# Sliding-window attention with a gated feed-forward layer: one third of the gate layer of five more token groups by seven half-size products

## The chip, the cores and the metric

The kernel runs on one core of a Trainium2 chip. The metric is the device time of one execution, in microseconds (us); smaller is better. The engines that matter: TensorE (PE in the profile, PEld its weight loads), VectorE (DVE), ScalarE (ACT), GpSimd (POOL, called Pool here) and SyncE (SP), which only issues transfers. The letter q behind an engine's name stands for its instruction queue.

## The reference, cut to what matters

```python
# B, H, S, D = 8, 8, 576, 64; window 128; float32 inputs
scores = (q @ k^T) / 8 + slope_h * -|i - j|,  only for 0 <= i - j < 128
attn   = softmax(scores)
x      = (attn @ v), heads side by side       # 4608 tokens x 512
gelu   = 0.5 * g * (1 + erf(g / sqrt 2)),  g = x @ w_gate     # 512 x 1536
out    = (gelu * (x @ w_val)) @ w_out         # 1536 x 512, float32
```

## The kernel before

The 4608 tokens form nine groups g = 0 to 8 of 512 tokens. For each group the *gates* compute the hidden layer in twelve blocks f = 0 to 11 of 128 columns (`gate_val`): four matmuls of 512 columns with `wg`, four with `wv`, a Gelu by ScalarE, and a multiply by VectorE that writes block f of `hT`. Below, "hT3" is that multiply of block 3. Then `out_products` (groups 2 and up) multiplies the hidden layer by `w_out`, by Strassen's scheme in Winograd's form: seven products of half size in each direction in place of eight, P(n, a) for token quarter a. They need sums of quarters of `hT`, which `combine_left` makes in the tile `left`: four steps, s1, s2, s4 and one in place (a21). P(1,0) and P(2,0) come first and read the quarters of `hT` for the first half of the tokens, P(1,0) the even blocks and P(2,0) the odd ones, so that the last matmul of P(2,0) needs hT11.

Between these products stands the attention of batch b = g + 2 (`scores2`, exponentials by ScalarE, masks by VectorE) and the weighting of V for batch g + 1. `add` then adds the masked probabilities into `T`, from which `sums4` makes the row sums early in the next group's gates; VectorE inverts them (`RECIPROCAL r<-ps`), `gather` writes them to DRAM and `spread_dma` reads them back to all partitions. Both of these transfers are issued from ScalarE's queue, ahead of whatever ScalarE does next.

The gates of some blocks use the same scheme of seven: `gate_quad(g, f0)` makes blocks f0 to f0 + 3 of both `wg` and `wv` by 56 matmuls of 256 columns. It needs sums of weight quarters (`combine_weights`), sums of token quarters (`combine_x`, four steps t1 to t4), six copies or adds from PSUM into a float32 staging place, and four Gelus. Its last multiplies are VectorE's for the first half of the tokens and Pool's for the second (`hidden(u, 1)`). In the kernel before it serves blocks 6 to 9 of group 1, and blocks 0 to 3 and 6 to 9 of groups 7 and 8. Its seven products come in the order 1, 2, 6, 5, 7, 3, 4; 6 accumulates onto 1 after ScalarE has copied 1 out, 4 onto 7 after VectorE has read that.

Every engine's instructions run in the order of the code (`manual_schedule`); nothing is reordered by a planner. A list `put_off` holds work that is emitted inside the next group's gates. Pool issues all loads of q, k and v (`load_qk`, `load_v`, 15 transfers for each batch, line 117), SyncE the transposes of q and k and the stores. Writes of a `mark` make Pool wait until something has happened before it goes on.

Of the kernel before, what the change touches and what calls it, by code (L numbers as in the profile page):

```python
# [7 lines left out]
FP32 = mybir.dt.float32  # L8
# [15 lines left out]
RING = 2048  # L24

QUADS = {0: 0, 6: 512}
# [10 lines left out]
def kernel(  # L37
# [60 lines left out]
    emask = consts.tile([128, H, 576], BF16, name="emask")  # L98
# [131 lines left out]
    def decay(s, c):  # L230
        return emask[:, 2 * c:2 * c + 2, 192 * s:192 * s + 384]
# [4 lines left out]
    def mask(dst, m):  # L236
        nc.vector.tensor_tensor(out=dst, in0=dst, in1=m, op=ALU.mult)  # L237
# [277 lines left out]
    def values_and_sums(b, s, later=None):  # L515
# [21 lines left out]
        def scale():  # L537
            for c, a, e, _, prods in two:
                at = b * S + a
                nc.vector.tensor_tensor(  # L540
                    out=xT[:, c, at:at + e - a], in0=prods, in1=recip[b][:, c, a:e], op=ALU.mult)
# [214 lines left out]
    def flat_of(t):  # L756
        return t.rearrange("p a x -> p (a x)")

    sums_w = [flat_of(t)[:, lo:lo + 2048].rearrange("p (c f) -> p c f", c=2)
              for t, lo in ((Ps[0], 0), (Ps[0], 2048), (Ps[0], 4096), (emask, 0))]  # L760

    def combine_weights(f0, to=None, engine=nc.gpsimd):
        todo = []
        if to is None:
            to = [t[:, :, QUADS[f0]:QUADS[f0] + 512] for t in sums_w]
# [9 lines left out]
    def sums_x(g):  # L775
        t, lo = (flat_of(left[:, :, :, :].rearrange("p n i x -> p (n i) x")), 2048) if g == 1 else (
            flat_of(T), 2048 * (g % 2))
        return [t[:, lo + 512 * n:lo + 512 * n + 512].rearrange("p (c x) -> p c x", c=2) for n in range(4)]
# [5 lines left out]
    def combine_x(g, lo=0, hi=256, which=range(4)):  # L784
# [3 lines left out]
        for n in which:  # L788
            to, a, b, op = steps[n]
            nc.vector.tensor_tensor(out=to, in0=a, in1=b, op=op)  # L790

    wide = [flat_of(t)[:, 1024 * i:1024 * i + 1024].bitcast(FP32)
            for t in (qT[0], kT[0], qT[1]) for i in (0, 1)]
    gelus = [flat_of(qs[0])[:, 512 * i:512 * i + 512] for i in range(4)]

    def early_space():
        slots = [Ps[0][:, 2 * n:2 * n + 2, 64:576] for n in range(4)]
        spare = r_pool.tile([128, 4, S], FP32, name="rb")
        staging = [spare[:, n, 0:512] for n in range(4)] + [
            flat_of(vb[1])[:, 1024 * i:1024 * i + 1024].bitcast(FP32) for i in (0, 1)]  # L800
        flat = flat_of(left[:, :, :, :].rearrange("p n i x -> p (n i) x"))
        return slots, staging, [flat[:, 512 * i:512 * i + 512] for i in range(4)]

    def gate_quad(g, f0, space=None):
        if g not in hid:
# [3 lines left out]
        slots, staging, gelu_tiles = space or (  # L809
            [t[:, :, QUADS[f0]:QUADS[f0] + 512] for t in sums_w], wide, gelus)  # L810
        s1, s2, s3, s4 = slots
# [20 lines left out]
        def add_to(n, to, u):  # L832
            nc.vector.tensor_tensor(out=to[u], in0=banks[n, u], in1=to[u], op=ALU.add)  # L833

        def gelu(what, frm, u):
            nc.scalar.activation(out=gelu_tiles[2 * what + u], in_=frm[u], func=AF.Gelu)  # L836

        def both(x):
            return x.rearrange("p (e x) -> p e x", e=2)
# [5 lines left out]
        for u in (0, 1):  # L845
            copy(out=P1[u], in_=banks["x", u])
# [4 lines left out]
        for u in (0, 1):  # L851
            copy(out=U[u], in_=banks["x", u])
        P(5)
        for u in (0, 1):
            copy(out=P5[u], in_=banks["y", u])
# [10 lines left out]
        for u in (0, 1):  # L866
            nc.vector.tensor_tensor(out=hidden(u, 0), in0=both(banks["x", u]), in1=both(gelu_tiles[u]), op=ALU.mult)
            nc.gpsimd.tensor_tensor(out=hidden(u, 1), in0=both(P5[u]), in1=both(gelu_tiles[2 + u]), op=ALU.mult)  # L868
# [107 lines left out]
    def masks_of_last_blocks(lo, hi):  # L976
        nc.vector.tensor_copy(out=emask[:, lo:hi, 192:384], in_=emask[:, lo:hi, 0:192])
        nc.vector.tensor_copy(out=emask[:, lo:hi, 384:512], in_=emask[:, lo:hi, 0:128])
        for x, at in ((0, 128), (1, 0)):
            half = slice(64 * x, 64 * x + 64)  # L980
            nc.vector.tensor_copy(out=emask[half, lo:hi, 512:576], in_=emask[half, lo:hi, at:at + 64])
# [156 lines left out]
    def out_products(g):  # L1138
# [106 lines left out]
        add(b, 0, None, (2, 1))  # L1245
        put_off.append(lambda: add(b, 2))

    put_off = []

    for g in range(NG):  # L1250
        if 1 <= g < B - 2:
            transposes_dma(3 if g == 1 else g + 2)
        if g >= B - 1:
            for f in range(NF):
                if f in QUADS:
                    if g == B - 1 and f == 0:
                        sums = combine_weights(6)
                        nc.gpsimd.tensor_copy(out=mark, in_=sums_x(g)[3][0:1, 1, 254:256])
                        for do in sums[:4]:
                            do()  # L1260
                    gate_quad(g, f)
                    if g == B - 1 and f == 0:
                        for do in sums[4:]:
                            do()
# [14 lines left out]
        if g == 1:  # L1279
            space = early_space()  # L1280
            sums = combine_weights(6, space[0], nc.vector)
            for do in sums[:5]:
                do()
        for f in range(9 if g == 0 else 0, NF):
            if g == 1 and 6 <= f < 10:
                if f == 6:
                    gate_quad(1, 6, space)
                continue
            gate_val(g, f)
# [5 lines left out]
            if g == B - 2 and f == 6:  # L1295
                combine_x(g + 1, 0, 192)
            if g == B - 2 and f in (2, NF - 1):
# [88 lines left out]
```

## Time and profile before

| | |
|---|---|
| median of 3 runs | 331.38 us (330.38 to 331.44) |
| the profiled execution | 331.55 us, its span 329.7 us |
| PE, DVE, ACT, POOL busy | 321.1, 261.4, 189.2, 148.0 us |
| granted TensorE clock | 1.0 throughout |
| chain that ended last | PE 93% |

All times of single instructions are microseconds from the start of the span of the profiled execution. Groups 3, 4 and 5 are alike: their gates begin at 133.29, 167.89 and 202.44 us.

### The profile page before, as it was taken

How to read it: one execution, taken by the hardware profiler on the slowest of the kernel's cores; microseconds unless marked ns; L12 is line 12 of the kernel's file. 1: busy time of each engine (PE TensorE's matmuls, PEld its weight loads, DVE VectorE, ACT ScalarE, POOL GpSimd, SP SyncE). 2: the span in 40 equal slices, each digit the busy share in tenths (PEclk: the TensorE clock that was granted, in tenths of full speed). 3: DMA queues.
4: the chain of work that ended last, by engine and by line, in shares of the span. 5: the costliest groups of instructions: out<-in, count | busy, mean ns of one | idle time of the engine just before them, and what ended most of it. 6: DMA issues, size and time to landing. Idle time of an engine off the chain costs nothing.

```text
span 329.7 us, 9178 instructions
## 1 busy us (share of the span) xinstructions
PE 321.1 (97%) x3664; PEld 204.4 (62%) x3664; DVE 261.4 (79%) x545; ACT 189.2 (57%) x371; POOL 148.0 (45%) x181
## 2 busy tenths in 40 slices
PE   8999999999999998999999999999999999999996
PEld 6566646574654466545854486447744787788764
DVE  7788686878779975989699769986899776886692
ACT  7974688567798365424842385237623247636641
POOL 5965589293095085105900392014014448910550
PEclk9999999999999999999999999999999999999999
DMA  8999999999999979969994599649201430003003
GB/s 214 168 195 191 202 170 168 145 190 154 135 179 154 165 139 196 167 151 166 173 184 128 138 155 156 153 139 133 99 33 45 104 130 2 0 2 128 2 0 127
DMA packets 149918, 43.54 MB, mean 132 GB/s; under 512 B 133588, under 2 KB 142964, under 8 KB 149876
## 3 DMA queue, kind: packets, MB, share of 16 engines
q0 software_dynamic: 107456, 18.10, 72.4%
q1 hardware_dynamic: 39104, 18.55, 26.7%
q10 hardware_dynamic: 3316, 6.32, 8.2%
q8 instruction: 28, 0.46, 0.5%
q14 instruction: 14, 0.11, 0.1%
HBM read 43.65 MB, written 9.53 MB: 161 GB/s over the span
## 4 chain that ended last, share of the span: by engine, by line
PE 93%; ACT 3%; DMA 1%; issue 1%; DVE 1%; ACTq 0%; DVEq 0%
PE ps L650 44%; PE ps L753 19%; PE ps L825 9%; PE ps L504 5%; PE ps L687 5%; PE ps L303 2%; PE ps L221 2%; PE ps L707 2%; ACT P L234 2%; DMA rd<-r 1%; PE ps L78 1%; PE ps L440 1%; PE ps L159 1%; PE ps L989 1%; PE ps L341 1%
## 5 line engine op out<-in xcount | busy, mean ns | idle before, releaser
L657 ACT ACTIVATE gelu<-ps 128x512 bf16<-128x512 f32 (+3 forms) x97 | 53.5, 557 | 80.1 <-PE ps L650 68.8
L650 PE MATMUL ps<-xT,wg 128*128 128x512 bf16 (+4 forms) x392 | 92.3, 357 | 0.0
L650 PE MATMUL ps<-xT,wv 128*128 128x512 bf16 (+4 forms) x392 | 92.2, 357 | 0.0
L658 DVE TENSOR_TENSOR hT<-ps,gelu 128x512 bf16<-128x512 f32 (+3 forms) x97 | 59.2, 633 | 17.6 <-PE ps L650 13.0
L650 PEld LDWEIGHTS <-wv 128*128 128x128 bf16 x392 | 37.2, 98 | 39.3 <-DVE xT L558 0.5
L650 PEld LDWEIGHTS <-wg 128*128 128x128 bf16 x392 | 36.5, 98 | 36.4
L234 ACT ACTIVATE P<-ps 128x512 bf16<-128x512 f32 (+1 forms) x108 | 52.3, 576 | 4.2 <-PE ps L221 2.1
L237 DVE TENSOR_TENSOR P<-P,emask 128x768 bf16<-128x768 bf16 x60 | 31.9, 553 | 7.2 <-ACT P L234 5.4
L753 PEld LDWEIGHTS <-hT 128*128 128x128 bf16 x336 | 31.9, 97 | 7.4 <-DVE hT L658 0.7
L117 POOL DMA_DIRECT2D vb<-in_v_dram x40 | 33.9, 888 | 3.6 <-DMA wo<-in_moe_w_out_dram 1.0
L1331 POOL COPY mark<-hT 1x2 bf16<-1x2 bf16 x4 | 1.5, 366 | 73.1 <-DVE hT L658 73.1
L117 POOL DMA_DIRECT2D ks<-in_k_dram x30 | 25.4, 889 | 4.4 <-DMA qs<-in_q_dram 4.2
L753 PEld LDWEIGHTS <-left 128*128 128x128 bf16 x252 | 24.2, 98 | 4.9 <-issue 1.6
L117 POOL DMA_DIRECT2D qs<-in_q_dram x30 | 25.2, 856 | 1.8 <-issue 1.2
L753 PE MATMUL ps<-right,hT 128*128 128x256 bf16 x168 | 22.2, 272 | 0.2 <-DVE osb L895 0.2
L753 PE MATMUL ps<-right,left 128*128 128x256 bf16 x168 | 20.6, 273 | 1.5 <-issue 1.5
L753 PE MATMUL ps<-wo,hT 128*128 128x256 bf16 x168 | 21.2, 273 | 0.4 <-DVE hT L658 0.4
L504 PE MATMUL ps<-P,vb 64*64 64x192 bf16 (+2 forms) x752 | 18.2, 221 | 1.6 <-issue 0.8
L868 POOL TENSOR_TENSOR hT<-qT,qs 128x512 bf16<-128x512 f32 x8 | 9.2, 1169 | 21.4 <-ACT qs L836 21.4
L504 PEld LDWEIGHTS <-vb 64*64 64x64 bf16 x752 | 14.9, 107 | 4.4 <-issue 3.6
L833 DVE TENSOR_TENSOR qT<-ps,qT 128x512 f32<-128x512 f32 x16 | 10.3, 686 | 8.5 <-PE ps L825 8.5
L687 PE MATMUL ps<-wo,hT 128*128 128x512 bf16 x72 | 16.9, 380 | 0.0
(158 smaller groups left out, 476.4 us busy)
## 6 DMA issues: line engine op xcount, KB each, us to landing
out_dram<-osb SPq DMA_DIRECT2D x34, 256.0 KB
rb<-rd ACTq DMA_DIRECT2D x10, 576.0 KB
vb<-in_v_dram POOLq DMA_DIRECT2D x32, 128.0 KB, 6.5
qs<-in_q_dram POOLq DMA_DIRECT2D x24, 128.0 KB, 5.8
ks<-in_k_dram POOLq DMA_DIRECT2D x24, 128.0 KB, 7.7
wo<-in_moe_w_out_dram POOLq DMA_DIRECT2D x4, 384.0 KB, 12.1
wg<-in_moe_w_gate_dram POOLq DMA_DIRECT2D x5, 256.0 KB, 9.5
wv<-in_moe_w_val_dram POOLq DMA_DIRECT2D x5, 256.0 KB, 10.1
```

The source lines that it names most:

```text
L117: nc.gpsimd.dma_start(out=t[at:at + n, j, :].rearrange("p (h d) -> p h d", h=H), in_=src[b][:, 128 * j:128 * j + n, :].rearrange("h p d -> ...
L234: nc.scalar.activation(out=dst, in_=src, func=AF.Exp, scale=0.125)
L237: nc.vector.tensor_tensor(out=dst, in0=dst, in1=m, op=ALU.mult)
L504: mm = nc.tensor.matmul(out=out, lhsT=lhsT, rhs=prob(b)[half, c, i, col:col + q1 - q0], start=all(t[2] != u for t in todo[:n]), stop=True, ...
L650: nc.tensor.matmul(out=ps[:, a:e], lhsT=w[:, c, 128 * f:128 * (f + 1)], rhs=xT[:, c, t0 + lo + a:t0 + lo + e], start=begins and a == 0, st ...
L657: nc.scalar.activation(out=gl[:, 0:n], in_=pg, func=AF.Gelu)
L658: nc.vector.tensor_tensor(out=hid[g][:, f, lo:hi], in0=pv, in1=gl[:, 0:n], op=ALU.mult)
L687: nc.tensor.matmul(out=acc[g], lhsT=hid[g][:, f, 128 * t:128 * (t + 1)], rhs=wo[:, f, :], start=(f == 0), stop=(f == NF - 1))
L753: nc.tensor.matmul(out=made[g, a, into], lhsT=lhsT, rhs=rhs, start=first and i == 0, stop=i == NF // 2 - 1, skip_group_check=True)
L825: nc.tensor.matmul(out=ps[:, 256 * e:256 * e + 256], lhsT=w[:, c, at:at + 128], rhs=x[:, c, :], start=n in (1, 2, 5) and e == 0 and c == 0 ...
L833: nc.vector.tensor_tensor(out=to[u], in0=banks[n, u], in1=to[u], op=ALU.add)
L868: nc.gpsimd.tensor_tensor(out=hidden(u, 1), in0=both(P5[u]), in1=both(gelu_tiles[2 + u]), op=ALU.mult)
```

## The change

`gate_quad(g, 6)` now serves groups 2 to 6 as well. What goes with it:

- The weight sums for blocks 6 to 9 are kept for good in a new tile `kept`, made once in group 1; those for blocks 0 to 3 are made by Pool after the gates of group 6. Room for it comes from a ring `xT` of 1536 tokens in place of 2048 and from a mask `emask` of 384 columns in place of 576.
- In groups 2 to 6 the token sums (`combine_x`) are made by Pool after hT3, followed there by the hidden layer's sums for pairs 0 to 2 of blocks (`combine_left`), then by the two `hidden(u, 1)` multiplies, then by the loads. Before, VectorE made all of these sums, and Pool's mark waited for hT9.
- VectorE makes the sums of pairs 3 and 4 (blocks 6 to 9) after hT10 and ahead of hT11.
- The copies in `add` (`what` 1) go from VectorE to ScalarE, at f = 0 and f = 2.
- `gather` is issued at f = 5 (before: f = 6, in group 2 f = 7), `spread_dma` behind the quad's instructions (before: f = 8, in group 2 f = 9).
- Staging for the quad is in `Ps[g % 2]` and `vb[g % 2]`, in group 6 in `qT`, `kT` and `qs`.

The core of the diff:

```diff
-RING = 2048
+RING = 1536
...
-        add(b, 0, None, (2, 1))
-        put_off.append(lambda: add(b, 2))
+        add(b, 0, None, (2,))
+        put_off.update({0: lambda: add(b, 0, act, (1,)), 1: lambda: add(b, 2, None, (0, 2)),
+                        2: lambda: add(b, 2, act, (1,))})
...
         for f in range(9 if g == 0 else 0, NF):
-            if g == 1 and 6 <= f < 10:
-                if f == 6:
-                    gate_quad(1, 6, space)
-                continue
-            gate_val(g, f)
+            if f == 6 and g:
+                gate_quad(g, 6, room if g == 1 else None)
+            elif not (g and 6 < f < 10):
+                gate_val(g, f)
...
-            if g == B - 2 and f == 6:
-                combine_x(g + 1, 0, 192)
-            if g in PRODUCTS and f in ((7, 9) if g == B - 2 else (7, 9, 11)):
-                combine_left(g, *{7: (0, 3), 9: (3, 5), 11: (5, 6)}[f])
-                if f == (7 if g == 2 else 6):
-                    gather(g + 1)
-                if f == (9 if g == 2 else 8):
-                    spread_dma(g + 1)
-                if f == 9 and g + 2 < B:
-                    nc.gpsimd.tensor_copy(out=mark, in_=hid[g][0:1, f, 0:2])
-                    if g + 3 < B:
-                        load_qk(g + 3)
+            if f == 3:
+                nc.gpsimd.tensor_copy(out=mark, in_=hid[g][0:1, f, 510:512])
+                combine_x(g, engine=nc.gpsimd)
+                combine_left(g, 0, 2, (0, 1, 3, 2), engine=nc.gpsimd)
+            if f == (5 if g == 2 else 4):
+                sums4(g + 1)
+            if f == 5:
+                combine_left(g, 2, 3, (0, 1, 3, 2), engine=nc.gpsimd)
+                gather(g + 1)
+                if g == B - 2:
+                    combine_x(g + 1, 0, 192)
+            if f == 6:
+                spread_dma(g + 1)
+                if g + 3 < B:
+                    load_qk(g + 3)
+                if g + 2 < B:
                     load_v(g + 2)
+            if f == 10:
+                combine_left(g, 3, 5, (0, 1))
+            if f == 11:
+                combine_left(g, 5, 6, (0, 1))
+                for n in (3, 2):
+                    combine_left(g, 3, 6, (n,))
+        if g == B - 2:
+            sums = combine_weights(0)
+            nc.gpsimd.tensor_copy(out=mark, in_=left[0:1, 2, 5, 0:2])
+            for do in sums:
+                do()
```

How the instructions stand now, at the places that the prediction rests on. "waits" names the engine or the transfer queue whose semaphore an instruction waits for.

Pool in the gates of group 3, before: the names are the mark, then the loads of q into `qs`.

```order
L1331 COPY mark<-hT 1x2 [waits DVE_49,Pool_49]
L117 DMA qs_95<-in_q_dram 128x8x64 [waits DMAHW4_49,DMASW1_49]
L117 DMA qs_95<-in_q_dram 128x8x64 [waits DMAHW5_49,DMASW2_49]
L117 DMA qs_95<-in_q_dram 128x8x64 [waits DMAHW6_49,DMASW3_49]
L117 DMA qs_95<-in_q_dram 128x8x64 [waits DMAHW7_49,DMASW4_49]
```

Pool at the same place now:

```order
L1325 COPY mark<-hT 1x2 [waits DVE_49]
L800 TENSOR_TENSOR left<-xT 128x512 [waits PE_49]
L800 TENSOR_TENSOR left<-xT,left 128x512 [waits Pool_49]
L800 TENSOR_TENSOR left<-xT 128x512 [waits PE_49]
L800 TENSOR_TENSOR left<-xT,left 128x2x256 [waits Pool_49]
L737 TENSOR_TENSOR left<-hT 128x512
L737 TENSOR_TENSOR left<-left,hT 128x512 [waits Pool_49]
L737 TENSOR_TENSOR hT<-hT 128x2x256
L737 TENSOR_TENSOR left<-hT,left 128x512 [waits Pool_49]
L737 TENSOR_TENSOR left<-hT 128x256 [waits DVE_49]
L737 TENSOR_TENSOR left<-left,hT 128x256 [waits Pool_49]
L737 TENSOR_TENSOR hT<-hT 128x256
```

Behind these follow one more sum of 128x256, the two `hidden` multiplies of 128x2x256, which wait for ScalarE's Gelus, and only then the loads: fourteen sums and multiplies have come between the mark and the first load.

VectorE at the end of the gates of group 3, before: `L658` are the multiplies hT10 and hT11, `L728` the sums of the last pair.

```order
L728 TENSOR_TENSOR left<-hT 128x512 [waits DVE_49]
L728 TENSOR_TENSOR left<-left,hT 128x512 [waits DVE_49]
L728 TENSOR_TENSOR left<-hT,left 128x512 [waits DVE_49]
L728 TENSOR_TENSOR hT<-hT 128x2x256
L658 TENSOR_TENSOR hT<-ps,gelu 128x512 [waits PE_49,Activation_49] x2
L728 TENSOR_TENSOR left<-hT 128x256 [waits DVE_49]
```

The same place now: `L881` are the quad's multiplies for the first half, `L667` is hT10 and then hT11.

```order
L881 TENSOR_TENSOR hT<-ps,vb_104 128x2x256 [waits DMASW4_49,PE_49,Activation_49]
L667 TENSOR_TENSOR hT<-ps,gelu 128x512 [waits PE_49,Activation_49]
L737 TENSOR_TENSOR left<-hT 128x512 [waits Pool_49]
L737 TENSOR_TENSOR left<-left,hT 128x512 [waits DVE_49]
L667 TENSOR_TENSOR hT<-ps,gelu 128x512 [waits PE_49,Activation_49]
L737 TENSOR_TENSOR left<-hT 128x256 [waits DVE_49]
```

hT11 now stands behind a sum that waits for Pool's second `hidden` multiply; before, nothing ahead of it waited for Pool.

ScalarE's row in the gates of group 3 before: `L657` are the Gelus (of blocks 1 to 6, 7, 8, and 9 to 11), `L453` the two transfers of `gather`, `L459` those of `spread_dma`.

```order
L657 ACTIVATE gelu<-ps 128x512 [waits DVE_49,PE_49] x6
L453 DMA rd<-r 2x8x128 [waits DMAHW0_49,DVE_49]
L453 DMA rd<-r 2x8x160 [waits DMAHW1_49,DVE_49]
L657 ACTIVATE gelu<-ps 128x512 [waits PE_49,Activation_49]
L657 ACTIVATE gelu<-ps 128x512 [waits DVE_49,PE_49]
L459 DMA rb<-rd 64x4x576 [waits DMAHW4_49,DMAHW2_49,DMAHW5_49,DMAHW1_49,DMAHW0_49]
L459 DMA rb<-rd 64x4x576 [waits DMAHW3_49]
L657 ACTIVATE gelu<-ps 128x512 [waits DVE_49,PE_49] x3
```

The same from block 5 on, now: `L457` is `gather`, `L860` to `L869` the quad's copies, `L853` its Gelus, `L463` is `spread_dma`, and the last row is the Gelus of blocks 10 and 11.

```order
L457 DMA rd<-r 2x8x128 [waits DMAHW0_49,DVE_49]
L457 DMA rd<-r 2x8x160 [waits DMAHW1_49,DVE_49]
L860 COPY P_106<-ps 128x2x256 [waits PE_49] x2
L866 COPY P_106<-ps 128x2x256 [waits PE_49] x2
L869 COPY P_106<-ps 128x4x128 [waits PE_49] x2
L853 ACTIVATE vb_104<-P_106 128x512 [waits DMASW5_49,DVE_49]
L853 ACTIVATE vb_104<-P_106 128x512 [waits DMASW6_49,DVE_49]
L853 ACTIVATE vb_104<-P_106 128x512 [waits DMASW7_49,DVE_49]
L853 ACTIVATE vb_104<-P_106 128x512 [waits DMASW0_49,DVE_49]
L463 DMA rb<-rd 64x4x576 [waits DMAHW4_49,DMAHW2_49,DMAHW5_49,DMAHW1_49,DMAHW0_49]
L463 DMA rb<-rd 64x4x576 [waits DMAHW3_49]
L666 ACTIVATE gelu<-ps 128x512 [waits PE_49,Activation_49] x2
```

`gather` has moved ahead of the quad's first copies, so these now stand behind its wait for VectorE's reciprocals, and the Gelu of block 10 stands behind `spread_dma`, which comes after the quad's last Gelu.

140 lines of the change are left out of this document (71 added, 69 removed).

## The prediction

> **What bounds the kernel now.** I read the page first: the engines' busy shares, then the chain of work in order of time, then the timelines of single engines in one group. The page's first line, and of the chain the group whose gates begin at 167.89:
>
> ```profile
> PE   321.1 (97%) x3664; PEld 204.4 (62%) x3664; DVE 261.4 (79%) x545; ACT 189.2 (57%) x371; POOL 148.0 (45%) x181
> ```
>
> ```profile
> 167.89 8.63 PE ps L650 x40
> 176.52 0.61 PE ps L440 x32
> 177.14 12.19 PE ps L650 x56
> 189.33 1.31 PE ps L753 x12
> 190.64 0.80 PE ps L303 x31
> ...
> 202.44 8.63 PE ps L650 x40
> ```
>
> Columns of the chain are start, length, what. TensorE works without a gap: 20.82 us of gates (L650), the row sums, then P(1,0) and P(2,0) (L753, 12 matmuls, 0.109 each), which end at 190.64. From gates to gates are 34.55 us. So TensorE bounds these groups, and any wait put in its way counts in full.
>
> **What the products save.** From the chain in group 7, a quad and two blocks of the plain kind:
>
> ```profile
> 269.31 6.11 PE ps L825 x56
> 275.42 3.45 PE ps L650 x16
> ```
>
> Four plain blocks are 2 x 3.45 = 6.90, a quad is 6.11: 0.79 less, over five groups 3.95 us. That quad ran with nothing in its way. The question is what the new work does to VectorE, ScalarE and Pool, and what TensorE then waits for. I follow group 4 (gates from 167.89).
>
> **VectorE.** Its timeline (start, length, engine, line, operation, counts):
>
> ```profile
> 171.48 0.79 DVE L397 COPY T<-P 64x1024 bf16<-64x1024 bf16 x2
> 172.30 1.29 DVE L658 TENSOR_TENSOR hT<-ps,gelu 128x512 bf16<-128x512 f32 x2
> 175.43 0.81 DVE L397 COPY T<-P 64x1024 bf16<-64x1024 bf16 x2
> 176.27 1.88 DVE L658 TENSOR_TENSOR hT<-ps,gelu 128x512 bf16<-128x512 f32 x3
> 178.07 1.96 DVE L445 RECIPROCAL r<-ps 128x128 f32<-128x128 f32 x2
> 186.71 0.42 DVE L728 TENSOR_TENSOR left<-hT 128x512 bf16<-128x512 bf16 x1
> 187.17 0.42 DVE L728 TENSOR_TENSOR left<-left,hT 128x512 bf16<-128x512 bf16 x1
> 189.44 0.69 DVE L658 TENSOR_TENSOR hT<-ps,gelu 128x512 bf16<-128x512 f32 x1 [0.45 <-PE ps L650]
> ```
>
> hT2, hT3 and hT4 share the fourth row, so hT3 ends at 177.5. The change takes both pairs of copies (0.79 + 0.81) off VectorE; hT3 then ends at about 175.9. It can't be before 175.5, because TensorE ends block 3 at 167.89 + 4 x 1.726 = 174.8. The reciprocals, ready when the row sums are at 177.14, end at 179.1 in place of 180.03. On balance VectorE gains six adds and two multiplies of the quad (some 0.68 each, as the multiplies), loses four multiplies, the copies and the sums of three pairs: it isn't its total that matters, but what its queue stands behind, below.
>
> **Pool.** Here is the cost that the diff hides. Pool's prices, from its timeline:
>
> ```profile
> 186.81 0.36 POOL L1331 COPY mark<-hT 1x2 bf16<-1x2 bf16 x1 [21.45 <-DVE hT L658]
> 195.60 4.28 POOL L117 DMA_DIRECT2D vb<-in_v_dram  x5
> 246.19 0.18 POOL L1302 COPY mark<-hT 1x2 bf16<-1x2 bf16 x1 [20.11 <-DVE hT L658]
> 246.34 2.25 POOL L770 TENSOR_TENSOR P<-wv 128x512 bf16<-128x512 bf16 x2
> 248.56 2.26 POOL L770 TENSOR_TENSOR P<-P,wg 128x512 bf16<-128x512 bf16 x2
> 282.66 1.16 POOL L728 TENSOR_TENSOR left<-hT 128x512 bf16<-128x512 bf16 x1
> 283.89 1.16 POOL L728 TENSOR_TENSOR left<-left,hT 128x512 bf16<-128x512 bf16 x1
> 285.54 2.32 POOL L868 TENSOR_TENSOR hT<-qT,qs 128x512 bf16<-128x512 f32 x2 [0.48 <-ACT qs L836]
> ```
>
> A sum of 128x512 takes Pool 1.13 (four from 246.34 to 250.82), against 0.42 on VectorE; where one reads the one ahead, 1.23 lie between the starts. After hT3 Pool does the mark (0.15 to the next start), eight sums of 128x512 (8 x 1.13 + 2 x 0.1 = 9.2), four of 128x256, and the two multiplies (2.3). The trace has no Pool sum of 128x256: at least half of the full one, 0.58, at most no cheaper, 1.13. I take 0.63, near the half, since the mark's 0.18 shows how little an almost empty instruction costs: 2.5. Together 14.15. So Pool's second multiply ends at 175.9 + 14.15 = 190.05, though the quad's data were ready well before.
>
> VectorE's sum of pair 3 and 4 waits for that multiply, and hT11 stands behind it: 190.05 + 0.42 + 0.46 + 0.69, with the semaphores 191.65. The last matmul of P(2,0) reads hT11, so P(2,0) ends at 191.75 in place of 190.64: **+1.1 us in a group, after the saving is used up**. In between lies the rest of TensorE's work, which doesn't fill the time: 0.79 less of gates and whatever the quad waits. Bounds for a group like this: hT3 at 175.5 and halves at 0.58 give +0.5; hT3 at 177.5 and halves at 1.13 give +4.7. Pool's order before had only the mark and loads here, and its idle 21.45 us in the row of 186.81 is what is being spent: as a share of time it has room, within the 12.5 us from hT3 to the end of the gates it hasn't.
>
> [...]
>
> **ScalarE.** Rows for the copies, the two transfers of `gather`, and the copy that moves here:
>
> ```profile
> 102.80 1.90 ACT L397 COPY T<-P 64x1024 bf16<-64x1024 bf16 x2 [0.49 <-DVE P L237]
> 179.93 1.14 ACTq L453 DMA_DIRECT2D rd<-r  x2
> 183.48 1.30 ACTq L459 DMA_DIRECT2D rb<-rd  x2
> 271.52 1.07 ACT L852 COPY kT<-ps 128x512 f32<-128x512 f32 x2 [0.62 <-PE ps L825]
> 273.60 1.15 ACT L836 ACTIVATE qs<-qT 128x512 bf16<-128x512 f32 x2
> ```
>
> A group adds six copies (0.6, the second of a pair 0.5 later), four Gelus for four plain ones, and the two pairs of copies out of `add` (1.90 each). These lie at f = 0 and f = 2, where ScalarE has a Gelu of 0.6 in each 1.73 of TensorE: both are done by 174.7, ahead of the row sums at 176.52, and I cost them at nothing; that cover goes if ScalarE comes more than 1.8 late into the gates.
>
> `gather` costs something. It waits for the reciprocals (179.1), takes 1.14, and the quad's first copy is done at 180.85. Product 6 wants the bank that this copy empties at 178.87 + 1.75 = 180.6, so it waits 0.25; with the next hand-overs between copies, adds and products the quad ends about 0.4 late, at 185.35 in place of 184.98. Behind it ScalarE's last two Gelus end 1.35 later, `spread_dma` takes 1.30, the Gelu of block 10 0.60: 188.6. Then on VectorE hT10 (0.69), the two sums (0.42 and 0.46), hT11 (0.69): 190.9. That is a second path to the end of P(2,0), at 191.0, only 0.75 ahead of Pool's. Since both meet at hT11, only the later counts, and the quad's own 0.4 is not added to the 1.1.
>
> **Group 2 and group 6** differ. Their rows on VectorE (the last two beside Pool's row of 285.54 above) and in the chain:
>
> ```profile
> 104.70 3.68 DVE L658 TENSOR_TENSOR hT<-ps,gelu 128x512 bf16<-128x512 f32 x6
> 108.30 1.96 DVE L445 RECIPROCAL r<-ps 128x128 f32<-128x128 f32 x2
> ...
> 245.37 1.89 DVE L658 TENSOR_TENSOR hT<-ps,gelu 128x512 bf16<-128x512 f32 x3
> ...
> 251.07 0.36 DVE L790 TENSOR_TENSOR T<-xT,T 128x384 bf16<-128x384 bf16 x1
> ...
> 286.51 0.34 DVE L728 TENSOR_TENSOR left<-hT 128x256 bf16<-128x256 bf16 x1
> 286.88 1.13 DVE L728 TENSOR_TENSOR left<-left,hT 128x256 bf16<-128x256 bf16 x1
> ```
>
> ```profile
> 107.53 3.57 PE ps L650 x16
> ...
> 118.92 0.94 PE ps L753 x7
> ...
> 258.43 3.27 PE ps L753 x30
> ```
>
> In group 2 VectorE comes late into the gates from group 1's work, which the change leaves as it is: hT3 ends at 104.70 + 4 x 0.61 = 107.15. Pool ends at 121.3, hT11 at 122.9, P(2,0) at 123.0 in place of 119.86: **+3.1**. The second path: `sums4` and `gather` both come at f = 5 here, the reciprocals end at 110.2, the copy at about 112, product 6 wanted it at 107.53 + 1.75 = 109.3. The quad ends near 116.0 in place of 113.64, and with the same 5.65 behind it P(2,0) ends at 121.7, +1.8.
>
> In group 6 hT3 ends at 246.6 - 1.6 = 245.0, which by the same sum gives 259.15 for Pool and 260.85 for P(2,0), in place of 258.43 + 1.31 = 259.74: +1.1. But here VectorE has four sums of `combine_x` (0.36 each) after hT5, in the middle of Pool's. The row of 286.88 took 1.13 for what took 0.29 to 0.34 elsewhere, and ended as Pool's second multiply did (285.54 + 2.32 = 287.86): sums of VectorE from SBUF alone and Pool's take turns. Bounds: no loss (+1.1), or each of the four waits out a Pool instruction, which puts VectorE 4 x 1.1 back ahead of the adds that product 4 waits for, and Pool 4 x 0.36 (about +4). I take +2.8, nearer the upper, since Pool runs without a gap there. [...] In groups 2 to 5 it costs nothing, since VectorE's other such sums stand ahead of hT3 in its queue, and Pool begins behind hT3.
>
> **Loads.** They now start behind Pool's second multiply, at 190.05 in place of 187.2 (mark and 0.4), so 3 us later; relative to the next gates 2 later. They end at 203, the next group's mark is wanted at 211. The transposes that read them:
>
> ```profile
> 170.73 6.51 SPq L187 DMA_TRANSPOSE qT<-qs  x5
> ```
>
> They are issued by 177.24 and wanted by the scores at 190.64, 13 us later: hidden. `spread_dma` comes some 3 later, at 186.7, its data are wanted after 200: hidden. Pool's eight weight sums after group 6 (9 us from about 264) are needed one by one by the first quad of group 7, 9.6 us after P(2,0); the last of them only by product 3, 4.4 further on: hidden. The masks from a smaller tile and the multiplies that the ring of 1536 splits in two in group 1 (some 0.3 on VectorE) I cost at nothing: group 1's end waits for neither.
>
> **Sum.** 3.1 + 3 x 1.1 + 2.8 = 9.2 on the profiled 331.55, which is 0.17 above the median: **340.6 us** against the median.
>
> **Rivals.**
> - *ScalarE's path ends the groups* (Pool is quicker than I think, as with twice VectorE's price): 1.8 + 3 x 0.35 + 2.8 = 5.7, 337.1. For it: 0.75 is all that parts the paths. Against: Pool's prices are measured. Chance 0.17.
> - *Both paths are hidden, and the 3.95 come in full*: 327.4. For it: TensorE's quads elsewhere ran with no gap. It decides when hT11 is done by 190.0 in group 4, so Pool's chain in at most 12.5 in place of 14.15, and the Gelu of block 10 a microsecond sooner. Chance 0.07; half way to it, within 0.3% (1.0 us) of before, which is about what a measurement can tell, 0.05.
> - *More is late than I see*: loads 3 us later meet a full DMA queue, or hT3 comes at its old time, so the paths cost 2 to 4 us a group: 345 to 350. Chance 0.11.
>
> The forecast has 0.60, from 338 to 344 by its own bounds. The range takes in the rival of ScalarE's path and part of the last one: 335 to 347. Faster 0.07, same 0.05, slower 0.88.
>
> **What would show it.** Gaps of TensorE ahead of the last matmul of P(2,0), of some 1.5 to 2 us in groups 3 to 5, longer in group 2; VectorE idle ahead of the sum of pair 3 and 4, released by Pool; Pool without a gap from the mark to its second multiply, 14 us; groups 3 to 5 35.6 us long. If Pool's chain measures under 12.5, or VectorE waits there for ScalarE's Gelu, the Pool step is wrong; if TensorE has no gap there, the whole forecast is.

## The result and the profile after

The changed kernel takes 345.18 us (median of 4 runs, 343.9 to 345.55), the kernel before 330.88 beside it: 1.0427 times the time before, interval 1.0395 to 1.0459. The profiled execution has a span of 342.8 us in place of 329.7, and its granted clock is 0.985 in place of 1.0. Where an experiment below has executions of over 1.5% above its fastest (both moves together, and Pool's eight sums in another order, whose profile is of one), its ratio leaves them out, while its median is of all.

From the page, the busy line and the shares of the chain that ended last, the chain's 93% PE of before being now:

```profile
PE 323.4 (94%) x3784; PEld 218.2 (64%) x3784; DVE 258.9 (76%) x516; ACT 220.2 (64%) x417; POOL 207.0 (60%) x242
PE 70%; POOL 15%; ACT 5%; DVE 4%; issue 4%; ACTq 0%; POOLq 0%; DVEq 0%
```

The chain of work in order of time (start, length, what), from the gates of group 4, which begin there at 172.64, to the products behind them:

```profile
177.00 0.60 ACT gelu L666
177.62 1.04 ACT T L401
...
179.54 0.61 ACT gelu L666
180.17 0.70 DVE hT L667
181.10 1.13 POOL left L800
...
193.94 1.16 POOL hT L887
195.13 0.44 DVE left L737
195.93 0.69 DVE hT L667
196.96 0.82 PE ps L307 x32
197.77 5.72 PE ps L762 x36
```

Where TensorE alone carried this stretch, the chain now leaves it at block 2 for ScalarE's Gelu, goes over the copies that the change moved to ScalarE (L401) and the Gelu of block 3 to hT3, then through Pool for 14 us, and over VectorE's sum of pairs 3 and 4 to hT11. The single engines there, Pool first (the mark, the first sum, the first of 128x256, the two multiplies, the first loads):

```profile
180.92 0.17 POOL L1325 COPY mark<-hT 1x2 bf16<-1x2 bf16 x1 [9.58 <-DVE hT L667]
181.06 1.15 POOL L800 TENSOR_TENSOR left<-xT 128x512 bf16<-128x512 bf16 x1
...
190.21 0.67 POOL L737 TENSOR_TENSOR left<-hT 128x256 bf16<-128x256 bf16 x1
...
192.83 2.27 POOL L887 TENSOR_TENSOR hT<-P,vb 128x512 bf16<-128x512 f32 x2
195.04 4.26 POOL L117 DMA_DIRECT2D qs<-in_q_dram  x5
```

VectorE (hT10, and the sum that waits for Pool):

```profile
192.48 0.69 DVE L667 TENSOR_TENSOR hT<-ps,gelu 128x512 bf16<-128x512 f32 x1 [1.04 <-ACT gelu L666]
195.13 0.43 DVE L737 TENSOR_TENSOR left<-hT 128x512 bf16<-128x512 bf16 x1 [1.96 <-POOL hT L887]
```

TensorE (eleven matmuls of P(1,0) and P(2,0), the twelfth, and the twelve of the next product but one):

```profile
193.12 1.36 PE L762 MATMUL ps<-wo,hT 128*128 128x256 bf16 x11
196.68 0.28 PE L762 MATMUL ps<-wo,hT 128*128 128x256 bf16 x1 [2.19 <-DVE hT L667]
197.71 2.74 PE L762 MATMUL ps<-right,left 128*128 128x256 bf16 x12
```

Pool works without a pause from 180.92 to 195.10; VectorE waits 1.96 us for it, TensorE 2.19. The third row holds what the prediction didn't reckon with: twelve matmuls take 2.74 us behind the gap, though they wait for nothing. In the windows that hold the gaps of groups 3 and 4, and the one behind the second (the granted clock is the number ahead of the last two):

```profile
159.00:164.00 5.00, 3.59 (x67) 3.00 (x68) 4.17 (x11) 2.77 (x7) 5.00 (x7) 1.00 1.72 156
196.00:200.00 4.00, 3.33 (x56) 2.49 (x57) 3.27 (x9) 1.57 (x3) 4.00 (x5) 0.70 1.72 144
200.00:204.00 4.00, 4.00 (x64) 3.19 (x65) 1.45 (x5) 2.53 (x7) 4.00 (x6) 0.87 2.28 143
```

Two rows of the chain of before that were not shown yet: an empty stretch of TensorE in group 2, behind the products of its first token quarters, and the 36 matmuls behind group 4's P(2,0):

```profile
126.47 1.47 issue
...
191.44 4.13 PE ps L753 x36
```

So these 36 take 5.72 in place of 4.13: 1.6 us lost in group 4, and the same in group 5. Group 3 has as long a gap (2.20) but kept its clock (1.00 over the 4 us from its end, against 0.62 and 0.60 in groups 4 and 5), and lost 0.28 at this place. Its chain shows why, the add of an output quarter behind VectorE's late sums and then 30 of its 36 matmuls:

```profile
161.88 0.34 DVE osb L911
162.26 3.51 PE ps L762 x30
```

So some 1.3 of the 1.6 are the clock's. The whole 13.1 us of span, counted along TensorE from gates to gates:

| part | groups | predicted | measured |
|---|---|---|---|
| end of P(2,0) later, counted from the gates | 2 | 3.1 | 3.87 |
| | 3, 4, 5 | 1.1 each | 1.52, 1.57, 1.56 |
| | 6 | 2.8 | 1.77 |
| between P(2,0) and the next gates | 2 | 0 | -1.35 |
| | 3, 4, 5 | 0 | 0.28, 1.60, 1.60 |
| | 6 | 0 | 0.17 |
| ahead of group 2, behind group 6 | | 0 | 0.43, 0.07 |
| sum | | 9.2 | 13.1 |

### The profile page after: what moved, and what is told of

It is laid out like the page before. It is cut to its first block, busy times and chain, and to the rows that moved or that the text cites. A ratio compares the mean times of both kernels' runs of the same rounds, so it can differ in the third digit from the quotient of the medians.

```text
span 342.8 us, 9509 instructions
## 1 busy us (share of the span) xinstructions
PE 323.4 (94%) x3784; PEld 218.2 (64%) x3784; DVE 258.9 (76%) x516; ACT 220.2 (64%) x417; POOL 207.0 (60%) x242
## 4 chain that ended last, share of the span: by engine, by line
PE 70%; POOL 15%; ACT 5%; DVE 4%; issue 4%; ACTq 0%; POOLq 0%; DVEq 0%
PE ps L659 23%; PE ps L762 18%; PE ps L842 11%; POOL left L737 6%; POOL left L800 5%; PE ps L508 5%; PE ps L696 5%; DVE hT L667 2%; PE ps L307 2%; PE ps L221 2%; PE ps L716 2%; ACT P L236 2%; POOL hT L887 2%; ACT gelu L666 1%; POOL hT L737 1%
## 5 line engine op out<-in xcount | busy, mean ns | idle before, releaser
L659 PE MATMUL ps<-xT,wg 128*128 128x512 bf16 (+4 forms) x312 | 71.8, 352 | 0.0
L659 PE MATMUL ps<-xT,wv 128*128 128x512 bf16 (+4 forms) x312 | 71.7, 352 | 0.0
L666 ACT ACTIVATE gelu<-ps 128x512 bf16<-128x512 f32 (+3 forms) x77 | 41.5, 546 | 35.4 <-PE ps L659 32.7
L667 DVE TENSOR_TENSOR hT<-ps,gelu 128x512 bf16<-128x512 f32 (+3 forms) x77 | 46.5, 622 | 18.1 <-PE ps L659 9.8
L659 PEld LDWEIGHTS <-wv 128*128 128x128 bf16 x312 | 29.4, 98 | 29.9 <-DVE xT L567 0.5
L659 PEld LDWEIGHTS <-wg 128*128 128x128 bf16 x312 | 28.8, 98 | 25.9
L842 PEld LDWEIGHTS <-kept 128*128 128x128 bf16 x256 | 25.8, 101 | 6.6 <-ACT P L860 3.0
L762 PE MATMUL ps<-right,left 128*128 128x256 bf16 x168 | 23.2, 294 | 0.1
L850 DVE TENSOR_TENSOR P<-ps,P 128x512 f32<-128x512 f32 x24 | 15.1, 684 | 10.0 <-PE ps L842 6.6
L842 PE MATMUL ps<-left,kept 128*128 128x256 bf16 x144 | 18.2, 287 | 2.7 <-ACT P L860 2.7
```

Of the source, the lines that this page charges most:

```text
L659: nc.tensor.matmul(out=ps[:, a:e], lhsT=w[:, c, 128 * f:128 * (f + 1)], rhs=xT[:, c, t0 + lo + a:t0 + lo + e], start=begins and a == 0, st ...
L666: nc.scalar.activation(out=gl[:, 0:n], in_=pg, func=AF.Gelu)
L667: nc.vector.tensor_tensor(out=hid[g][:, f, lo:hi], in0=pv, in1=gl[:, 0:n], op=ALU.mult)
L762: nc.tensor.matmul(out=made[g, a, into], lhsT=lhsT, rhs=rhs, start=first and i == 0, stop=i == NF // 2 - 1, skip_group_check=True)
L842: nc.tensor.matmul(out=ps[:, 256 * e:256 * e + 256], lhsT=w[:, c, at:at + 128], rhs=x[:, c, :], start=n in (1, 2, 5) and e == 0 and c == 0 ...
```

## The experiments

In each, "the changed kernel" is the edited one; its groups are measured from gates to gates, and a ratio is to the kernel before on the same chip. Gaps and lengths are those of the profiled execution.

### The sums of pairs 3 and 4 behind hT11

```diff
-            if f == 10:
-                combine_left(g, 3, 5, (0, 1))
             if f == 11:
-                combine_left(g, 5, 6, (0, 1))
+                combine_left(g, 3, 6, (0, 1))
```

> The sums of pairs 3 and 4 go behind hT11 on VectorE; Pool's work is as before. Theory A (TensorE waits for hT11, which stands behind a wait for Pool's second multiply, and the 2.2 us gap then lowers TensorE's clock in groups 4 and 5): no gap ahead of the last matmul of P(2,0), hT11 done near +21.3 us from the start of the gates in place of +24.0; the wait comes back smaller in front of P(6,0), some 0.8 us, since Pool's second multiply still ends near +22.5, and the copy of product 6 behind the late sums costs some more; the clock stays at 1.0. About 1.1 us less in each of groups 3 to 5, 3.2 less from the clock, about 1 less in groups 2 and 6: 337 us. Rival B (ScalarE's path through gather, the quad's copies, spread_dma and the Gelu of block 10 ends the group): hT11 is no earlier than +23.5, the time falls by less than 2 us. Rival C (the slow products after the gap come from something other than the gap, such as Pool's loads running beside them): they stay at some 0.22 us each in groups 4 and 5.

338.06 us, 1.0188 (1.0147 to 1.0229). Nothing waits ahead of P(2,0) in groups 3 to 5, which are 35.3 us long in place of 36.4 to 37.7, and in the rows of groups 3 and 4 no matmul is slower: six of a product take 0.81 to 0.83, as in the kernel before. TensorE's timeline, group 3:

```profile
160.41 0.50 PE L762 MATMUL ps<-right,left 128*128 128x256 bf16 x3 [0.50 <-DVE left L737]
161.68 0.81 PE L762 MATMUL ps<-right,left 128*128 128x256 bf16 x6 [0.77 <-DVE osb L911]
```

The wait of 2.2 has become 0.50 for a sum and 0.77 for an add that stands behind these sums. So hT11's place behind Pool was what cost, and moving it buys some 7 of the 14 us, the clock's part included.

### Token sums at the group's start

```diff
+            if f == 0:
+                combine_x(g, engine=nc.gpsimd)
             if f == 3:
                 nc.gpsimd.tensor_copy(out=mark, ...)
-                combine_x(g, engine=nc.gpsimd)
```

> Pool's four token sums are issued at block 0, ahead of the mark for hT3, where Pool was idle; everything else as in the changed kernel. Theory A: Pool's chain behind hT3 is 4.6 us shorter, so its second multiply ends near +18.5 to +19.5 from the start of the gates in groups 3 to 6 and hT11 is bounded by ScalarE's path, near +22; gap ahead of the last matmul of P(2,0) at most 0.5 us, clock 1.0. Against it, the token sums now take turns with VectorE's adds and masks at the start of the gates, which may move hT3 up to 2 us later. Groups 3 to 5 some 1.5 less each, the clock 3.2 less, group 6 1 less, group 2 little: 335 us, 333 to 339. Rival B (ScalarE's path): within 2 us of the changed kernel. Rival C (no clock effect of the gap): the waits go but the products stay slow, 340.

338.07 us, 1.0198 (1.0153 to 1.0243). Pool's chain is short enough: P(2,0) waits no longer in groups 3 to 5 (34.8 to 35.2 us each). But group 2 grew to 41.87, 2.6 more than in the changed kernel. VectorE's rows there (the adds into `T`, a copy, then the multiplies), and TensorE's wait:

```profile
103.03 3.54 DVE L391 TENSOR_TENSOR T<-P 64x1024 bf16<-64x1024 bf16 x2
106.58 1.07 DVE L395 COPY T<-P 64x256 bf16<-64x256 bf16 x1
...
108.86 3.68 DVE L667 TENSOR_TENSOR hT<-ps,gelu 128x512 bf16<-128x512 f32 x6
```

```profile
109.61 1.43 PE L659 MATMUL ps<-xT,wv 128*128 128x512 bf16 x4 [3.55 <-DVE hT L667]
```

At this place of the changed kernel the two adds took 1.39 and the copy 0.22, here 3.54 and 1.07, with nothing moved but Pool's four sums; that they take turns with these is my reading. The multiplies that TensorE needs stand behind them. Behind hT3, where the change puts them, Pool's sums stood clear of these; earlier they don't.

### Matmuls on zeros in the gap

```diff
+            if n == 1 and a == 0 and 2 <= g < 7:
+                keep_busy(made[g, a, into], 28 if 3 <= g < 6 else 8, 128)
```

> TensorE gets matmuls of zeros ahead of P(1,0) in groups 2 to 6 (8, 28, 28, 28 and 8 of 128 columns, into a bank that P(1,0) then begins anew), which fill most of its wait; their output is not used. Theory A with the clock as its second half: P(2,0) ends when it did (+24.3 in groups 3 to 5), the gap shrinks to under 0.8 us, and the products after it run at 0.109 us each in groups 4 and 5: 3.2 us less, 341.7 us. Rival C (the slow products have another cause than the gap): the time of the changed kernel, 345, or more by what the zeros delay.

339.89 us, 1.0238 (1.0201 to 1.0274). With matmuls of zeros put ahead of P(1,0), P(2,0) ends as long after the gates as in the changed kernel (24.4 us), but the gap is 0.62 in place of 2.19. Group 4, the rows that answer to 196.68 and 197.71:

```profile
194.08 0.28 PE L764 MATMUL ps<-wo,hT 128*128 128x256 bf16 x1 [0.62 <-DVE hT L667]
195.10 1.48 PE L764 MATMUL ps<-right,left 128*128 128x256 bf16 x12
```

1.48 in place of 2.74: more work on TensorE, and groups 4 and 5 are 1.6 us shorter each, group 3, which had kept its clock, 0.2. That is the clock, shown (its mean over the run is 0.998, in the changed kernel 0.985). The other 2 us of the difference lie ahead of group 2 (1.2) and in its wait for the quad's first copy (1.6 in place of 2.75), both ahead of the first of these matmuls; they aren't put down to them.

### Half as many zeros

The same with 14 and 4 matmuls in place of 28 and 8.

> As the run with zeros ahead of P(1,0), with half as many (4, 14, 14, 14 and 4), so that the gap ahead of the last matmul of P(2,0) is some 1.4 us in groups 3 to 5, between 0.6, which left the clock alone, and 2.2, which lowered it in two groups of three. If the gap's length decides at somewhere near 2 us, the products behind it stay at 0.109 us: 340 us. If any gap over 1 us can lower the clock, one or more of the groups shows products at some 0.22 us, 1.6 us each: 341.5 to 345.

341.46 us, 1.0319 (1.03 to 1.0339).

```profile
196.86 0.28 PE L764 MATMUL ps<-wo,hT 128*128 128x256 bf16 x1 [1.42 <-DVE hT L667]
197.88 1.72 PE L764 MATMUL ps<-right,left 128*128 128x256 bf16 x12
```

Behind gaps of 1.42 and 1.43 the clock fell in none of the three groups (twelve matmuls in 1.71 to 1.72 in each, granted 1.00 from 160 to 164 and from 196 to 200; all 36.3 to 36.4 long, against 37.7 where it fell). The 0.24 above 1.48 come at a granted clock of 1.0: the seventh of the twelve starts at 198.78, as VectorE's add behind the late sums ends, which is group 3's 0.28 again. So at this place gaps of 1.4 us left the clock alone in all three groups, and gaps of 2.2 lowered it in two of the changed kernel's three.

### Both moves together

> The token sums early on Pool and the sums of pairs 3 and 4 behind hT11. Theory A: neither hT11 nor the sums are late; no gap over 0.4 us, the clock at 1.0, and of the 0.79 us that a quad saves about 0.4 is left in a group of 3 to 5, less what the turns with VectorE's sums cost; group 2 keeps its 2.7 us wait for the first copy: 329 to 333 us, beside 331 before the change. Rival B: 337 or more, since ScalarE's path would still end each group late.

338.52 us, 1.0119 (1.0071 to 1.0168): by the ratio some 2 us less than with either move alone, though the intervals overlap, and more than the 329 to 333 expected. In its profile, of the execution of 338.52, groups 3 to 5 are 34.6, 35.3 and 35.3 us long, against 34.6, 34.6 and 34.5 before. VectorE's masks for the attention, and TensorE's quad in group 4:

```profile
173.04 2.85 DVE L241 TENSOR_TENSOR P<-P,emask 128x768 bf16<-128x768 bf16 x2
```

```profile
184.52 2.83 PE L842 MATMUL ps<-left,kept 128*128 128x256 bf16 x24 [0.70 <-POOL hT L737]
```

The profile names Pool for that wait, but Pool's sum had long been done; late are the quad's copies, behind `gather`, which waits for the reciprocals, which the two masks (2.85 us, one is 0.55 alone) have put back beside Pool's early sums. The run with the token sums early has the same wait in groups 4 and 5, 0.70 and 0.66. Group 2's wait of 2.80 for the first copy is that of the changed kernel (2.75). Here ScalarE's path, second by 0.75 in the prediction, was next in line.

### `gather` alone behind the quad's copies

```diff
-                gather(g + 1)          # at f == 5
...
+        if mid:                        # in gate_quad, behind its six copies
+            mid()
```

> Only gather is moved behind the quad's six copies; Pool's and VectorE's order is that of the changed kernel. Theory A (Pool's chain ends the groups): the 2.75 us wait for the first copy in group 2 goes, and yet P(2,0) ends when it did in every group, +24.3 us from the start of the gates in groups 3 to 5; the wait ahead of its last matmul grows by what the quad is faster; the time is that of the changed kernel, 343 to 345.5, with the clock lower after the gap in more groups if anything. Rival B (ScalarE's path ends them): P(2,0) 1 us earlier or more in group 2 and 0.3 in groups 3 to 5, 341 us or less.

345.67 us, 1.0442 (1.0412 to 1.0472): nothing gained, though group 2's wait of 2.75 for the first copy is gone (0.52 is left there, for a sum of Pool's). From TensorE's timeline in group 2, and the chain in group 3:

```profile
122.22 0.39 PE L762 MATMUL ps<-wo,hT 128*128 128x256 bf16 x1 [2.93 <-DVE hT L667]
```

```profile
162.18 5.78 PE ps L762 x36
```

The wait has gone over to hT11: Pool alone sets the end of P(2,0), in group 2 too. Here the clock fell behind the gaps of 2.20 in all of groups 3 to 5 (twelve matmuls took 2.56, 2.74 and 2.74; 0.79 was granted from 160 to 164), in the changed kernel behind those of groups 4 and 5 and not of group 3: five of six, and behind the 2.93 above as well (twelve in 2.74).

### A repaired version

`gather` behind the quad's copies; Pool's hidden sums only for pairs 0 and 1; VectorE makes those of pairs 2 to 5 behind hT11, the later steps each only ahead of the product that reads it.

```diff
+                combine_left(g, 2, 6, (0, 1))      # at f == 11
...
         O("c11", 0)
+        combine_left(g, 2, 6, (3,))
...
         O("u2", 0, dve)
+        combine_left(g, 2, 6, (2,))
```

> Three repairs at once. Pool keeps the token sums and the sums of pairs 0 and 1, so its chain behind hT3 is 2.6 us shorter; VectorE makes the sums of pairs 2 to 5 behind hT11, the last two steps of them behind the first copies out of P(2,0) and P(6,0); gather stands behind the quad's copies on ScalarE. Theory A (the three waits shown so far, for Pool, for the copies behind gather, and for the copies behind the late sums, are all that eats the quad's 0.79 us): groups 3 to 5 take 33.9 to 34.2 us each beside 34.55 before the change and 36.4 to 37.7 in the changed kernel, the clock stays at 1.0, in all 328 to 331 us, just under the time before. Rival B (something else in the engines' shares is at its limit, such as VectorE as a whole): a new wait of over 0.5 us shows in each group and they stay above 34.6.

330.76 us (12 runs), 1.0003 (0.9974 to 1.0033). All the waits of groups 3 to 5 are gone; they are 34.02 us long, 0.52 to 0.59 under before. Group 2, with a wait of 1.05 for hT11, is 36.62 (before 36.74). The most that is left stands in group 6 (33.55, before 32.32), ahead of a matmul that needs hT11 and of one that needs a sum:

```profile
257.08 0.94 PE L762 MATMUL ps<-wo,hT 128*128 128x256 bf16 x7 [0.49 <-DVE hT L667]
259.20 1.27 PE L762 MATMUL ps<-right,left 128*128 128x256 bf16 x10 [0.97 <-DVE left L737]
```

So the quads do pay in groups 3 to 5 once nothing waits for Pool, by the greater part of the 0.79 each; group 6 gives 1.2 of these 1.6 us back.

### The same with group 2's gates as before

> The repaired version with group 2's gates as before the change (twelve plain blocks, gather at block 7, loads at block 9). Theory A: group 2 is short of slack because VectorE comes late into it, so its quad gains nothing there; without it group 2 takes what it took before, 36.9 us with its gap of 1.5 at the scores or 35.4 without, and groups 3 to 6 keep 33.9 to 34.2: 328 to 330 us. If group 2's quad was as good as the others', 0.4 us more than the repaired version.

331.63 us, 1.0021 (1.0000 to 1.0042), above the 328 to 330 expected. Group 2 is 36.97 us long in place of 36.62 with its quad, before 36.74. But group 2 with its quad, the same code, took 36.62 to 38.73 in the profiles of the repaired version and of the three versions below, so whether the quad gains or costs there is not shown. Group 3 took 35.02 in place of 34.02, most of it a stretch of 0.74 in which TensorE waited for nothing that the profile shows.

### VectorE's token sums for group 7 later

The repaired version, with the four sums moved from f = 6 of group 6 to behind the sums that its products need.

```diff
-                if g == B - 2:                     # at f == 6
-                    combine_x(g + 1, 0, 192)
...
             combine_left(g, 2, 6, (2,))
+            combine_x(g + 1, 0, 192)
             sums = combine_weights(0)
```

> As e5_repaired, but VectorE's four sums of the next quad's tokens (for group 7) are made in group 6 behind the last of the sums that the products need, no longer ahead of hT10. In e5_repaired they took 2.1 us of VectorE ahead of hT10 (0.40 + 1.20 + 0.34 + 0.35), and group 6 was 33.55 us long, with waits of 0.49 for hT11 and 0.97 for a sum. Theory: these waits come from VectorE's queue; without the four sums hT11 and the sums come some 2 us sooner, both waits go, group 6 is 32.3 to 32.7 us long, the four sums take turns with Pool's weight sums (up to 1.2 us each), which nothing waits for, and the kernel takes 329.5 to 330, ratio 0.996 to 0.998. Rival: hT11 waits for ScalarE's Gelu of block 11 behind the quad's, and nothing is gained: 330.7, ratio 1.000.

340.56 us, 1.0299 (1.0252 to 1.0346): 10 us slower than the version it was to improve. VectorE (the first two of the four sums, and the add behind them), Pool (its eight weight sums) and the chain on TensorE behind:

```profile
260.51 0.35 DVE L800 TENSOR_TENSOR T<-xT 128x384 bf16<-128x384 bf16 x1
260.89 9.08 DVE L800 TENSOR_TENSOR T<-xT,T 128x384 bf16<-128x384 bf16 x1
...
270.44 0.41 DVE L919 TENSOR_TENSOR osb<-ps,osb 128x256 f32<-128x256 f32 x1
```

```profile
260.86 2.25 POOL L778 TENSOR_TENSOR P<-wv 128x512 bf16<-128x512 bf16 x2
...
267.51 2.25 POOL L778 TENSOR_TENSOR P<-wg,P 128x512 bf16<-128x512 bf16 x2
```

```profile
270.90 7.75 PE ps L762 x54
```

One sum that takes 0.35 lasted 9.08, from the start of Pool's row to its end. "Up to 1.2 each", expected for taking turns, was wrong: it got no turn in eight of Pool's instructions. The add behind it held TensorE up for 8.33 us, and the 54 matmuls behind that took 7.75, against 6.08 in the last run below (mean granted clock 0.99 here, 0.999 there).

### Pool's eight sums in another order

```diff
-        return [do for pair in zip(*todo) for do in pair]
+        return [do for half in todo for do in half] if f0 == 0 else ...
```

> As e9_x7_late, but Pool makes its eight weight sums in the order 1, 2, 3, 4 of the first half and then of the second, so that the second and the sixth of them read the one just ahead of them; in e9_x7_late no sum read the one just ahead, all eight ran from 260.86 to 269.73 without a pause, and VectorE's second token sum, begun at 260.89, took 9.08 us, to the end of the eighth. Theory A: VectorE's sum from SBUF alone is shut out until Pool pauses, as Pool does (some 0.1 us) ahead of a sum that reads the one just ahead. Then that sum ends behind Pool's first, after 1.2 to 1.5 us, a later one of the four may wait for Pool's fifth (4.5 to 5 us), and the longest of the four is at most 5.5 us; the kernel is 1 to 4 us faster than e9_x7_late. Theory B: VectorE gets no turn while Pool has any instruction ready: one sum takes 9 us again, and the time is that of e9_x7_late, 340.6.

333.46 us, 1.0075 (1.0044 to 1.0106), 7 us less than the version above, where theory A gave 1 to 4. VectorE's same sums:

```profile
263.79 1.33 DVE L800 TENSOR_TENSOR T<-xT,T 128x384 bf16<-128x384 bf16 x1
265.04 1.30 DVE L800 TENSOR_TENSOR T<-xT 128x384 bf16<-128x384 bf16 x1
266.27 1.30 DVE L800 TENSOR_TENSOR T<-xT,T 128x384 bf16<-128x384 bf16 x1
```

1.33 in place of 9.08, by nothing but the order on Pool, in which the second sum reads the first: theory B is out. A fits the first turn; for the next two it doesn't, since they came one after each of Pool's sums, also where Pool's next does not read the one ahead. In the changed kernel's group 6 even the first turn came without a pause of Pool's (the sum of 260.25 further down, between Pool's sums of 259.94 and 261.19). So the order decides here, and by what rule isn't settled.

### Pool's weight sums behind VectorE's token sums

```diff
-            nc.gpsimd.tensor_copy(out=mark, in_=left[0:1, 2, 5, 0:2])
-            for do in sums:
+            nc.gpsimd.tensor_copy(out=mark, in_=sums_x(g + 1)[3][0:1, 0, 0:2])
+            for do in sums[:6]:
                 do()
...
             combine_x(g + 1, 192, 256)
+            nc.gpsimd.tensor_copy(out=mark, in_=sums_x(g + 1)[3][0:1, 0, 192:194])
+            for do in sums[6:]:
+                do()
```

> As e9_x7_late, but Pool's first six weight sums wait for the last of VectorE's four token sums, and its last two for the four sums of the remaining 64 tokens. Theory (the 10 us of e9_x7_late are that one shut-out VectorE sum and nothing else): VectorE's four sums take 0.35 each again, no VectorE sum is over 1.6 us there, group 6 is 32.3 to 33.0 us long, the first quad of group 7 may wait up to 0.8 for a sum, and the kernel takes 329.5 to 330.8, ratio 0.996 to 1.001. Rival: the later place of the four sums costs by itself (an add behind them on VectorE, for which product 7 waits): 332 or more.

329.9 us, 0.9989 (0.9967 to 1.001); the four sums take 0.35 each again, the mean granted clock is 0.999, and group 6 is 32.77 us long.

```profile
261.00 0.36 DVE L800 TENSOR_TENSOR T<-xT,T 128x384 bf16<-128x384 bf16 x1
```

```profile
262.67 6.08 PE ps L762 x54
```

The 10 us were that one shut-out sum. This is the best version found, and its interval doesn't part it from the kernel before: by its profile groups 3 to 5 gain 1.6 us together, and groups 2 and 6 give back 0.4 each. In group 6 the rival of the run before the last two was half right: without the token sums VectorE waits 1.07 for the Gelu of block 10, which stands behind `spread_dma`, and TensorE 0.85 for one of VectorE's sums. In group 2 VectorE waits 3.05 for that Gelu, and TensorE 1.40 for hT11.

## Why the prediction was right or wrong

- **The time.** Slower was right, and so was the wait that makes it so. The size was not: 345.18 lies above the 338 to 344 of the forecast's own bounds, and inside 335 to 347 only because that range takes in part of the rival *More is late than I see*. Neither cause named there came about: hT3 was not at its old time, 9.6 us from the gates, but at 8.2, and TensorE waited for no load. So there was luck in it, helped by two errors the other way, 1.35 in group 2 and 1.0 in group 6.
- **The saving** of 0.79 a group is there in the repaired versions (0.52 to 0.59 of it) and is hidden in the changed one, as said. (The rival in which it comes in full set hT11 at 190.0 and the chain at 12.5; with 0.79 taken from 190.64 it is 189.7 and 12.2.)
- **Pool's chain**: forecast 14.15, measured 195.10 - 180.92 = 14.2. The 128x512 sums took 1.15 with 1.11 between starts, the 128x256 ones 0.67, 0.63 between starts, which the prediction had chosen between 0.58 and 1.13 without a row for it. That Pool takes twice VectorE's price, the case that the rival of ScalarE's path names, no run shows: Pool's 1.15 stands beside VectorE's 0.43 for a sum of 128x512 (`left` from `hT`), 2.7 times as much.
- **The +1.1 of groups 3 to 5** was 1.55. Counted from the gates in the chain, hT3 ended at 8.2 (forecast 8.0), Pool's second multiply at 22.5 (22.2), P(2,0) at 24.3 (23.9): no one step is off by more than 0.2. That moving hT11 ahead of Pool's sum takes the wait away, and moving `gather` does not, is shown by two runs, so the mechanism stands and the rival of ScalarE's path is out as a cause. As the next in line it was real.
- **The clock is the term that was missing.** I priced a gap at its own length. Behind it groups 4 and 5 lost 1.60 more, and group 3, with its clock up, 0.28: the clock's part is some 1.3 in each of the two, 2.6 of the 3.9 by which the sum of 9.2 falls short of 13.1. The rest is the end of P(2,0) in groups 3 to 5 (0.45 each), the add (0.3 each) and 0.5 outside these groups, less what groups 2 and 6 stay under their forecast (1.4 together). At this place twelve matmuls took 2.74 where the clock fell, against 1.48 behind the gap of 0.62; it fell behind gaps of 2.2 us five times in six, and behind gaps of 1.4 in none of three.
- **Group 2** was 3.87 and not 3.1, but 1.35 came back behind: TensorE's empty 1.47 at 126.47 of before, which waited for nothing the profile shows, is gone (the run with plain gates there has 1.39 of it). The forecast put the two paths 1.3 apart there, and they came closer: VectorE's wait for Pool ahead of hT11 was 0.27, but `gather` moved alone left Pool's. The clock accounts for that: it fell behind the wait for the quad's first copy too (0.61 over the 4 us from 112.57), and the quad ended 1.5 later by it. Its 24 matmuls there, and group 4's:

```profile
112.57 4.31 PE L842 MATMUL ps<-left,kept 128*128 128x256 bf16 x24 [2.75 <-ACT P L860]
...
185.31 2.78 PE L842 MATMUL ps<-left,kept 128*128 128x256 bf16 x24
```

- **Group 6** was 1.77 and not 2.8. VectorE's token sums do take turns with Pool, but the two sides don't pay alike:

```profile
260.25 1.20 DVE L800 TENSOR_TENSOR T<-xT,T 128x384 bf16<-128x384 bf16 x1
```

  Three of the four took 1.20 to 1.31 in place of 0.35, while Pool's took 1.27 to 1.29 in place of 1.15, so Pool lost 0.12 a turn, not 0.36. My upper bound took VectorE's full length from Pool, and I had chosen a value near it.
- **Costed at nothing.** ScalarE's copies out of `add` (1.87 to 1.90 a pair) are not quite hidden: the second pair stands ahead of the Gelu of block 3 and so on the chain to hT3, Pool and TensorE's gap. They cost about 0.1 us, though, since VectorE, behind its own adds, was ready only at 180.10 for the hT3 that began at 180.17. The loads, the lateness of `spread_dma`, the weight sums behind group 6 and the smaller ring and mask stand behind no wait of TensorE's in these groups.

## What to carry to other kernels

Before handing work to an engine with idle time, follow the chain from what releases it to who next waits for its last result: here 14 us of Pool had to fit into 12.5, and one multiply in VectorE's queue stood behind the answer. A gap of TensorE can cost more than its length: here gaps of 2.2 us cost 1.3 to 1.4 on top in five cases of six and gaps of 0.62 and 1.42 nothing, so shortening one from 2.2 to 1.42 gained more than the time it took out. Keep VectorE's sums of two SBUF tiles out of a row of Pool's that runs without a pause, or let Pool's row wait for them: here one took 9.08 us inside such a row, and 0.36 when the row waited.

## What the runs showed of the hardware that was not expected

- Gaps of 2.2 us ahead of the last matmul of P(2,0) lowered TensorE's granted clock in five of six cases (0.62 and 0.60 over the 4 us behind the two in the changed kernel), at 1.3 to 1.4 us each beyond the gap; gaps of 0.62 and 1.42 in the same place did not (twelve matmuls took 1.48 and 1.72, in place of 2.74). Elsewhere in TensorE's rows the matmuls behind gaps of 0.97 to 1.72 were no slower for them: the quad's 24 took 2.78 to 2.83, and 1.00 was granted over the 4 us behind the 1.47 of the kernel before and behind a 1.37 in group 6 of the changed one. Of 13 gaps of 2.18 to 8.33 eleven were followed by slower matmuls (24 in 4.30 to 4.49, twelve in 2.56 to 2.74), and two were not (2.20 in group 3 of the changed kernel, and 2.80 with both moves, where the 24 took 2.83). So the length alone doesn't decide, and what else does isn't settled.
- A VectorE sum from SBUF alone, 0.36 when Pool waited, lasted 9.08 us beside eight Pool sums in a row, and with the order of the eight changed 1.33.
- A copy was slower too: VectorE's in group 2 took 1.07 with Pool's four sums moved to the group's start, 0.22 at the same place of the changed kernel.
